# Stage D's casts on ScalarE, one relu and two accumulator sums at other places of their queues

## The chip, the cores and the metric

The kernel runs on one core of one Trainium2 chip. A core has TensorE (PE), VectorE (DVE), ScalarE (ACT), GpSimd (POOL) and SyncE (SP, which here only issues DMAs). Each engine works through its own queue of instructions in order; semaphores make one wait for another. The metric is device time of one execution in microseconds, as the median of several runs.

## The reference

Three layers, one behind the other. Input x is 8 x 3072 x 256 in fp32.

```
X  = rfft(x, axis=1)
Yr = Xr @ w_r - Xi @ w_i + b_r ;  Yi = Xr @ w_i + Xi @ w_r + b_i
Y  = soft threshold of Yr and Yi by 0.01
x  = irfft(Y)                                  # 24576 tokens of 256
x  = (relu(x @ moe_w_in) ** 2) @ moe_w_out     # 256 -> 2048 -> 256, 24576 tokens
logits = x @ phi                               # 32 slots
d  = softmax of logits over the tokens ;  slot_input = d.T @ x
slot_out = per expert (8): relu(slot_input @ w1) @ w2
out = softmax of logits over the slots @ slot_out
```

## The kernel before

The program has three parts: the transform (to about 530 us), the loop over units that holds the two matrix products of the middle layer and the sums over tokens (to about 2065 us), and a short end for the experts and the output. The change touches the loop only.

The 24576 tokens are cut into 32 super-blocks (`sb`) of 768. For each super-block 8 units (`r = n % 8`) are worked through; a unit is 256 of the 2048 hidden channels. A unit multiplies 2 x 2 blocks by seven products, p0 to p6, and each product is three matmuls (128 x 384, line 701), since the numbers are split into a high and a low part: `yh` (the value rounded to fp32r) and `yl` (the rest). The products of one unit are accumulated in two PSUM banks, `psA` and `psX`, with a third, `psZ`, for p4. ScalarE copies `psA` into `psX` (L708 behind p0, L716 behind p5) and `psZ` into SBUF (L722). Of the four results, called parts 0 to 3, parts 1 and 3 are made by VectorE as `psA` or `psX` plus the copy of `psZ` (`add(1)`, `add(3)`, line 735). All are passed through a relu on ScalarE (L739) and squared in place (L743; mostly by GpSimd, part 0 by VectorE). Then TensorE takes them to the logits (`ls`, L754), and VectorE transposes them in pairs into `gt` (`turn(1)` for parts 2 and 3, `turn(0)` for 0 and 1, L747).

The order on all engines is written out by hand in the loop over `n`. In one pass the unit `cur` (n) does p0, p1 and p5, the unit `p1` (n-1) does p4, p6, p2 and p3, and the unit `p2` (n-2) its transpositions and logits. (`p1` and `p2` as objects of the code are units; p1 and p2 as products are methods of the same name.) On TensorE a pass reads p0, p4, p6, p1, p5, p2, p3, logits. p1 needs L708's copy of `psA` into `psX`; p3 writes into `psX` and so needs `add(3)`, which reads it, to be over.

Three things hang in this loop besides:

- Stage D of the next super-block (`stage_d`, the decoding), a generator of which `step(r, k)` takes k pieces at the given r. It does an inverse transform on TensorE (`psY`), copies it to SBUF by ScalarE (four copies, L476; tensors f0 to f3 in the code), and from that makes the seven `yh` and `yl`: seven casts (L480), seven subtractions (L482) and four differences (L464), all on GpSimd.
- The slot run (`into_slots`, L765): at the end of r = 3, TensorE sums the tokens of the super-block before into slots, in four banks (`pz_a`, `pz_x` and two `pz`). The pass r = 4 that follows has another order, and there VectorE adds the banks to `acc` by four `collect` (L770).
- The weights of the slot run: at r = 2 VectorE takes `scores` and `lowest`, ScalarE `exponents` (L821, L822); at r = 3 there is a softmax over the slots (`over_slots`, L778 to L788) with one exponential on ScalarE (L782).

The lines that matter for ScalarE's order at r = 2:

```
step(2, 2)            # the last two copies of stage D
...
p1.p6()
p1.add(3, p1.x)
...
p1.relu(3)
```

Of the kernel before, what the change touches and what calls it, by code (L numbers as in the profile page):

```python
# [103 lines left out]
def fft_moe_kernel(ctx, tc, x, w_r, w_i, b_r, b_i, moe_w_in, moe_w_out, moe2_phi, moe2_w1, moe2_w2,  # L104
                   c_f1, c_bm, c_cm, c_dm, c_st, out):
    nc = tc.nc
# [6 lines left out]
    def f(ap):  # L113
        return ap.bitcast(F32)
# [10 lines left out]
    def drain(it):  # L125
        for _ in it:
            pass
# [312 lines left out]
    def load_z(s):  # L440
        t = zp.tile([128, TB, DM], F32, tag="zt", name=f"zt{s}")
        for g in range(2):
            b, c = divmod(2 * s + g, NC)
            nc.sync.dma_start(t[64 * g:64 * g + N1], zd[b][:, c])
        zt[s] = t

    def stage_d(s, bank, eng):

        yh = yp[s % 2].tile([128, 7, TOK], F32R, tag="yh", name=f"yh{s}")
        yl = yp[s % 2].tile([128, 7, TOK], F32R, tag="yl", name=f"yl{s}")  # L450
        yt[s] = (yh, yl)
        def fill(dh):
            ps = [bank(f"psY{s}_{dh}_{g}")[:, :TOK] for g in range(2)]
            for tt in range(TB):
                for g in range(2):
                    for c in range(2):
                        d = 128 * dh + 64 * c
                        w = slice(64 * g, 64 * g + N1)
                        nc.tensor.matmul(ps[g][64 * c:64 * c + 64, tt::TB], lhsT=zt[s][w, tt, d:d + 64], rhs=dmt[w],  # L459
                                         start=True, stop=True)  # L460
            return ps

        def sub(o, k, m):
            eng.tensor_tensor(out=o, in0=k, in1=m, op=ALU.subtract)  # L464

        if s not in zt:
            load_z(s)
            for _ in range(4):
                yield
        z = zt[s].rearrange("p t d -> p (t d)")  # L470
        f0, f2, f1, f3 = (v[:, o:o + TOK] for v, o in ((wgf, OY), (wgf, OY + TOK), (z, 0), (z, TOK)))
        for dh, ts in enumerate(((f0, f2), (f1, f3))):
            ps = fill(dh)
            yield
            for t, p in zip(ts, ps):
                nc.scalar.copy(t, p)  # L476
                yield
        for j, t, ns in ((0, f0, ((f0, f2, f0),)), (4, f0, ()), (2, f3, ()), (1, f1, ((f2, f3, f2),)),
                         (6, f2, ((f2, f3, f0), (f0, f2, f1))), (5, f2, ()), (3, f0, ())):
            eng.tensor_copy(yh[:, j], t)  # L480
            yield
            eng.tensor_tensor(out=yl[:, j], in0=t, in1=f(yh[:, j]), op=ALU.subtract)  # L482
            yield
            for n in ns:
                sub(*n)
                yield

    XB, XL = 4, NB * NC
    with tc.manual_schedule():
# [155 lines left out]
        def bank(name):  # L645
            return psM.tile([128, 512], F32, tag="g", name=name, bufs=2)

        def bank_a(m, name):
            return psM.tile([128, 512], F32, tag=f"a{m % 2}", name=name)
# [118 lines left out]
        def collect(s, a, p):  # L768

            nc.vector.scalar_tensor_tensor(out=acc[:, :, a], in0=acc[:, :, a], scalar=al[s],  # L770
                                           in1=p.rearrange("p (t n) -> p t n", n=32), op0=ALU.mult, op1=ALU.add)
# [37 lines left out]
        def scores():  # L809
            for h in range(2):  # L810
                w = slice(64 * h, 64 * h + 64)
                nc.vector.tensor_tensor(out=lw[w], in0=lgp[w, HT * h:HT * h + HT], in1=lv[w], op=ALU.add)

        def lowest(s):
            nc.vector.tensor_reduce(out=bx, in_=lw, axis=AX.X, op=ALU.max)
            nc.vector.scalar_tensor_tensor(out=nm[(s + 1) % 3], in0=bx, scalar=-1.0, in1=nm[s % 3], op0=ALU.mult, op1=ALU.min)
# [15 lines left out]
        def turn_rows():  # L832
            nc.vector.transpose(lts, lw)
            return lts.rearrange("p (k n) -> p k n", n=32)
# [52 lines left out]
            nc.tensor.matmul(p, lhsT=ident, rhs=acc.rearrange("p t a n -> p (t a n)")[:, :TOK], start=True, stop=True)  # L887
        units = {}
        NM = NSB * NW
        run = side = None  # L890
        for n in range(NM + 2):
            sb, r = divmod(n, NW)
            s = sb - 1 if sb > 0 and n < NM else None
            cur = units[n] = Unit(n) if n < NM else None
            p1, p2 = units.get(n - 1), units.get(n - 2)

            def step(at, k):

                if side is not None and r == at:
                    for _ in range(k):  # L900
                        next(side, None)

            def route(at):
                return s is not None and r == at

            if run is None:
                if cur:
                    cur.p0()
                step(1, 1)
                if p1:  # L910
                    p1.p4()
                step(1, 1)
                if route(2):
                    scores()
                    lowest(s)
                    exponents(s)
                step(2, 2)
                if p2 and r != 2:
                    p2.turn(1)
                if p1:  # L920
                    p1.p6()
                    p1.add(3, p1.x)
                if route(2):
                    weights(s)
                if p2 and r == 2:
                    p2.turn(1)
                if cur:
                    cur.p1()
                    cur.p5()
                if p2 and r not in (2, 3):  # L930
                    p2.turn(0)
                if p1:
                    p1.p2()
                    p1.add(1, p1.a)
                if p2 and r in (2, 3):
                    p2.turn(0)
                step(1, 1)
                if p1:
                    p1.relu(3)
                    p1.square(3, nc.gpsimd)  # L940
                    p1.p3()
                    p1.square(2, nc.vector if n == NM else nc.gpsimd)
                    p1.relu(1)
                    p1.square(1, nc.vector if n == NM else nc.gpsimd)
                if cur:
                    cur.square(0, nc.vector)
                if route(3):
                    cur.p4()
                    cur.p6()
                    drain(over_slots(turn_rows()))  # L950
                    keep(s, co)
                if p2:
                    p2.logits()
            else:
                sr, ps = run
                run = None
                p2.logits()
                p1.p3()
                p1.square(3, nc.gpsimd)
                p1.square(2, nc.gpsimd)  # L960
                collect(sr, 0, ps[0])
                collect(sr, 1, ps[1])
                cur.p0()
                p1.p2()
                p1.add(1, p1.a)
                collect(sr, 2, ps[2])
                p1.relu(1)
                p1.square(1, nc.gpsimd)
                collect(sr, 3, ps[3])
                cur.p1()  # L970
                cur.p5()
                cur.square(0, nc.gpsimd)
                p2.turn(1)
                p2.turn(0)
            if p1 and p1.s == NSB - 1:
                free_wi(p1.q)
            if n >= NM:
                continue
            if route(1):
                apart()  # L980
            if route(3):
                total(s)
            if r == 0 and sb + 1 < NSB:
                side = stage_d(sb + 1, bank, nc.gpsimd)
                next(side)
            step(2, 3)
            step(3, 10)
            step(4, 1)
            step(5, 2)
            step(6, 3)  # L990
            if r == 5 and sb + 2 < NSB:
                load_z(sb + 2)
            if route(3):
                ps = [bank_a(n + 1, f"pz{s}_a"), bank_x(n + 1, f"pz{s}_x")] + [bank(f"pz{s}_{i}") for i in range(2)]
                into_slots(s, ps)
                cur.add(3, cur.x)
                cur.relu(3)
                run = (s, ps)
            if sb == NSB - 1 and r == 0:
                t = zp.tile([128, TB, DM], F32, tag="zt", name="ez").rearrange("p t d -> p (t d)")  # L1000
                for k in range(2):
                    load_w1(t[:, FE * k:FE * k + FE])
                load_wo()
# [37 lines left out]
        ps = [bank_a(i, f"pz_a{i}") for i in range(2)] + [bank_x(i, f"pz_x{i}") for i in range(2)]  # L1041
# [33 lines left out]
    with ExitStack() as p3, tc.manual_schedule():  # L1075
# [12 lines left out]
        for e in range(e0, NE):  # L1088
            t = wk.tile([128, NX, DM], F32, tag=f"w2{e}", name=f"w2{e}")
# [44 lines left out]
        late = over_slots(lt)  # L1134
# [86 lines left out]
```

## Time and profile before

| | |
|---|---|
| median of 3 runs | 2180.7 us (2176.5, 2181.17, 2180.7) |
| the profiled execution's own time | 2177.24 us |
| its span | 2175.0 us |
| TensorE busy | 2080.6 us (96%) |
| VectorE busy | 1543.0 us (71%) |
| GpSimd busy | 1317.5 us (61%) |
| ScalarE busy | 1277.2 us (59%) |
| mean granted clock of TensorE | 0.977 |

A stretch of the span is best read by the timeline of each engine: start, duration, what ran, and in brackets how long the engine stood idle before it and for whom. The end of a matmul is modelled, so the distance between two starts is the safer number on TensorE. On the other engines instructions overlap a little: the next can start before the duration of the last is over.

### The profile page before, as it was taken

The numbers are of one execution on the slowest core, as the hardware profiler recorded it, in microseconds if no ns is written. First come the engines' busy times: TensorE is split into PE (matmuls) and PEld (weight loads), VectorE is DVE, ScalarE is ACT, GpSimd is POOL, SyncE is SP. The second block draws the span as 40 slices with busy tenths as digits, with TensorE's granted clock in tenths as the row PEclk, the third lists the DMA queues.
The fourth block names the chain that finished last, engine by engine and source line by source line (L and its number), as shares of the span: only waits on it lengthen the run. The fifth ranks groups of instructions, "written<-read, shape, count | busy, mean of one in ns | idle before, by whom it ended". The sixth has DMA issues, their size and how long they took to land.

```text
span 2175.0 us, 55408 instructions
## 1 busy us (share of the span) xinstructions
PE 2080.6 (96%) x22294; PEld 1598.3 (73%) x22294; DVE 1543.0 (71%) x2590; ACT 1277.2 (59%) x2910; POOL 1317.5 (61%) x1583
## 2 busy tenths in 40 slices
PE   8999999998899999999999999999999999999994
PEld 3888888887777777777777777777777777777743
DVE  2677677766577777777777777777777777777743
ACT  2667666754565566566556665655666666556632
POOL 0243344411777777777777777777777777777500
PEclk7999999998999999999999999999999999999995
DMA  8988898863011111111111111111111111111589
GB/s 245 263 242 238 232 231 235 237 152 94 16 36 27 29 36 32 27 27 32 31 29 30 39 27 27 29 34 29 27 41 27 27 27 36 29 27 46 169 302 396
DMA packets 113772, 210.02 MB, mean 97 GB/s; under 512 B 14092, under 2 KB 80908, under 8 KB 107244
## 3 DMA queue, kind: packets, MB, share of 16 engines
q1 hardware_dynamic: 112348, 203.31, 34.6%
q8 instruction: 175, 2.87, 0.6%
q10 hardware_dynamic: 1168, 3.18, 0.4%
q14 instruction: 81, 0.66, 0.1%
HBM read 122.64 MB, written 83.79 MB: 95 GB/s over the span
## 4 chain that ended last, share of the span: by engine, by line
PE 69%; DVE 13%; DMA 5%; ACT 4%; POOL 4%; issue 4%; SPq 1%; DVEq 0%; ACTq 0%; POOLq 0%
PE psX L701 14%; PE psA L701 12%; PE ls L754 7%; DVE gt L747 4%; PE psZ L701 4%; PE pz_a L765 4%; PE psB L247 4%; PE psC L331 4%; PE psY L459 3%; PE pz_x L765 3%; POOL wg L743 3%; PE pz L765 3%; DVE wg L735 3%; PE psA L214 2%; ACT wg L739 2%
## 5 line engine op out<-in xcount | busy, mean ns | idle before, releaser
L743 POOL TENSOR_TENSOR wg<-wg 128x384 f32<-128x384 f32 x797 | 707.3, 910 | 371.3 <-ACT wg L739 368.9
L747 DVE STREAM_TRANSPOSE gt<-wg 128x768 f32<-128x768 f32 x512 | 487.9, 962 | 172.2 <-POOL wg L743 171.9
L739 ACT ACTIVATE wg<-psX 128x384 f32<-128x384 f32 x512 | 251.8, 492 | 269.4 <-PE psX L701 217.6
L701 PE MATMUL psX<-yh,wia 128*128 128x384 f32 x1024 | 364.9, 356 | 39.1 <-DVE wg L735 36.1
L701 PE MATMUL psA<-yh,wia 128*128 128x384 f32 x1024 | 362.2, 359 | 0.0
L739 ACT ACTIVATE wg<-wg 128x384 f32<-128x384 f32 x512 | 267.8, 523 | 139.7 <-DVE wg L735 139.6
L701 PEld LDWEIGHTS psA<-yh,wia 128*128 128x128 f32 x1024 | 192.3, 188 | 103.4 <-DVE wg L735 42.6
L701 PEld LDWEIGHTS psX<-yh,wia 128*128 128x128 f32 x1024 | 192.5, 188 | 95.8 <-DVE wg L735 56.6
L123 POOL TENSOR_TENSOR Sl<-Sf,Sh 128x256 fp32r<-128x256 f32 x96 | 75.4, 786 | 274.2 <-ACT Sh L122 239.8
L754 PE MATMUL ls<-wg 128*32 128x384 f32 x2048 | 219.6, 499 | 0.3 <-DVE wg L743 0.3
L765 PE MATMUL pz_x<-gt,wg 32*32 32x512 f32 x1584 | 209.2, 597 | 0.0
L765 PE MATMUL pz_a<-gt,wg 32*32 32x512 f32 x1584 | 208.9, 596 | 0.0
L765 PE MATMUL pz<-gt,wg 32*32 32x512 f32 x2976 | 203.5, 597 | 0.0
L743 DVE TENSOR_TENSOR wg<-wg 128x384 f32<-128x384 f32 x227 | 195.8, 863 | 7.8 <-ACT wg L739 7.7
L708 ACT COPY psX<-psA 128x384 f32<-128x384 f32 x256 | 119.6, 467 | 120.1 <-PE psA L701 119.7
L701 PE MATMUL psA<-yl,wia 128*128 128x384 f32 x512 | 172.4, 337 | 0.0
L701 PE MATMUL psZ<-yh,wib 128*128 128x384 f32 x512 | 172.1, 336 | 0.0
L701 PE MATMUL psX<-yl,wia 128*128 128x384 f32 x512 | 172.0, 336 | 0.0
L701 PE MATMUL psX<-yh,wib 128*128 128x384 f32 x512 | 171.6, 335 | 0.0
L701 PE MATMUL psA<-yh,wib 128*128 128x384 f32 x512 | 171.5, 335 | 0.0
L735 DVE TENSOR_TENSOR wg<-psX,wg 128x384 f32<-128x384 f32 x256 | 137.1, 536 | 42.5 <-ACT wg L722 32.0
L735 DVE TENSOR_TENSOR wg<-psA,wg 128x384 f32<-128x384 f32 x256 | 136.1, 532 | 41.0 <-PE psA L701 39.0
(211 smaller groups left out, 4807.5 us busy)
## 6 DMA issues: line engine op xcount, KB each, us to landing
bt<-ad SPq DMA_DIRECT2D x96, 256.0 KB
zd<-sc SPq DMA_DIRECT2D x96, 256.0 KB
zt<-zd SPq DMA_DIRECT2D x64, 384.0 KB
xt<-in_x_dram SPq DMA_DIRECT2D x126, 192.0 KB
ad<-sa SPq DMA_DIRECT2D x112, 192.0 KB
out_dram<-ob SPq DMA_DIRECT2D x21, 1024.0 KB
wg<-ed SPq DMA_DIRECT2D x124, 96.0 KB
w<-in_moe_w_dram SPq DMA_DIRECT2D x5, 1024.0 KB
```

Of the source, the lines that this page charges most:

```text
L123: (eng or nc.vector).tensor_tensor(out=lo, in0=v, in1=f(hi), op=ALU.subtract)
L247: nc.tensor.matmul(p[:, dh, :, l], lhsT=t[:, l, 128 * dh:128 * dh + 128], rhs=bm[:, 2 * (u % NU) + l], start=True, stop=True)
L331: nc.tensor.matmul(ps[l][:, v], lhsT=cm[w, (u - 1 + v) % NU, c], rhs=ub[v][w, c], start=c == 0, stop=c == 1)
L459: nc.tensor.matmul(ps[g][64 * c:64 * c + 64, tt::TB], lhsT=zt[s][w, tt, d:d + 64], rhs=dmt[w], start=True, stop=True)
L701: nc.tensor.matmul(p, lhsT=w[:, k, l], rhs=r[:, j], start=start and n == 0, stop=n == 2, skip_group_check=True)
L708: nc.scalar.copy(self.x, self.a)
L735: nc.vector.tensor_tensor(out=self.part(k), in0=p, in1=self.z, op=ALU.add)
L739: nc.scalar.activation(out=t, in_=t if p is None else p, func=AF.Relu)
L743: eng.tensor_tensor(out=t, in0=t, in1=t, op=ALU.mult)
L747: nc.vector.transpose(gt[:, 2 * self.q + a + window(self.s)], self.g[a])
L754: nc.tensor.matmul(lgp[o:o + 32], lhsT=pw[:, 2 * self.q + a], rhs=self.part(k), start=self.first, stop=self.last, skip_group_check=True)
L765: nc.tensor.matmul(ps[a][32 * c:32 * c + 32], lhsT=ee[w, c, k], rhs=gt[w, o:o + NT2, 32 * j:32 * j + 32], start=k == 0, stop=k == NB6 - 1, ...
```

## The change

Four edits, all in stage D and in the loop over units.

1. The seven casts L480 of a super-block's stage D run on ScalarE where stage D ran on GpSimd (31 super-blocks; the first one's stage D runs on VectorE and stays).
2. The last two copies of stage D, which stood early in the pass r = 2, stand at its end, with the first cast behind them (`step(2, 5)`).
3. At r = 2 relu(3) stands right behind the sum add(3).
4. In the pass behind a slot run (r = 4) collect 2 stands ahead of add(1), and collect 3 stands at the end of the pass r = 5.

```diff
--- before.py
+++ after.py
@@ -477,7 +477,7 @@
                 yield
         for j, t, ns in ((0, f0, ((f0, f2, f0),)), (4, f0, ()), (2, f3, ()), (1, f1, ((f2, f3, f2),)),
                          (6, f2, ((f2, f3, f0), (f0, f2, f1))), (5, f2, ()), (3, f0, ())):
-            eng.tensor_copy(yh[:, j], t)
+            (eng.tensor_copy if eng is nc.vector else nc.scalar.copy)(yh[:, j], t)
             yield
             eng.tensor_tensor(out=yl[:, j], in0=t, in1=f(yh[:, j]), op=ALU.subtract)
             yield
@@ -887,7 +887,7 @@
             nc.tensor.matmul(p, lhsT=ident, rhs=acc.rearrange("p t a n -> p (t a n)")[:, :TOK], start=True, stop=True)
         units = {}
         NM = NSB * NW
-        run = side = None
+        run = side = late = None
         for n in range(NM + 2):
             sb, r = divmod(n, NW)
             s = sb - 1 if sb > 0 and n < NM else None
@@ -914,12 +914,13 @@
                     scores()
                     lowest(s)
                     exponents(s)
-                step(2, 2)
                 if p2 and r != 2:
                     p2.turn(1)
                 if p1:
                     p1.p6()
                     p1.add(3, p1.x)
+                if p1 and r == 2:
+                    p1.relu(3)
                 if route(2):
                     weights(s)
                 if p2 and r == 2:
@@ -936,7 +937,8 @@
                     p2.turn(0)
                 step(1, 1)
                 if p1:
-                    p1.relu(3)
+                    if r != 2:
+                        p1.relu(3)
                     p1.square(3, nc.gpsimd)
                     p1.p3()
                     p1.square(2, nc.vector if n == NM else nc.gpsimd)
@@ -952,7 +954,7 @@
                 if p2:
                     p2.logits()
             else:
-                sr, ps = run
+                sr, ps = late = run
                 run = None
                 p2.logits()
                 p1.p3()
@@ -962,11 +964,10 @@
                 collect(sr, 1, ps[1])
                 cur.p0()
                 p1.p2()
+                collect(sr, 2, ps[2])
                 p1.add(1, p1.a)
-                collect(sr, 2, ps[2])
                 p1.relu(1)
                 p1.square(1, nc.gpsimd)
-                collect(sr, 3, ps[3])
                 cur.p1()
                 cur.p5()
                 cur.square(0, nc.gpsimd)
@@ -983,7 +984,9 @@
             if r == 0 and sb + 1 < NSB:
                 side = stage_d(sb + 1, bank, nc.gpsimd)
                 next(side)
-            step(2, 3)
+            if late and r == 5:
+                collect(late[0], 3, late[1][3])
+            step(2, 5)
             step(3, 10)
             step(4, 1)
             step(5, 2)
```

VectorE from the slot run of super-block 1 on, the passes r = 4 and r = 5, as a piece of the difference. L770 is a collect (`pz_a`, `pz_x`, `pz_0`, `pz_1` are its banks 0 to 3), L735 with `psA` is add(1), with `psX` add(3), L747 a transposition, L743 the square of part 0; the number behind `psA_` or `psX_` is the group of channels of the unit:

```order
 L770 SCALAR_TENSOR_TENSOR acc<-acc,al_7570,pz_x 128x16x32
+L770 SCALAR_TENSOR_TENSOR acc<-acc,al_7570,pz_0_7693 128x16x32
 L735 TENSOR_TENSOR wg<-psA_1_7618,wg 128x384
-L770 SCALAR_TENSOR_TENSOR acc<-acc,al_7570,pz_0_7693 128x16x32
+L747 STREAM_TRANSPOSE gt<-wg 128x768 x3
+L735 TENSOR_TENSOR wg<-psX_2_7806,wg 128x384
+L747 STREAM_TRANSPOSE gt<-wg 128x768
+L735 TENSOR_TENSOR wg<-psA_2_7805,wg 128x384
+L743 TENSOR_TENSOR wg<-wg 128x384
 L770 SCALAR_TENSOR_TENSOR acc<-acc,al_7570,pz_1_7694 128x16x32
-L747 STREAM_TRANSPOSE gt<-wg 128x768 x3
```

Collect 2 (`pz_0`) moved up by one instruction, ahead of add(1), and collect 3 (`pz_1`) down by seven, behind the square of r = 5; transpositions and add(3) stand two instructions closer to add(1).

ScalarE in the pass r = 2 of super-block 1, from the second exponential to the copy L708 of r = 3. L476 are the two copies of stage D, L739 from `wg` to `wg` is a relu of part 3 or 1, L739 from `psX` of part 0 or 2. Before:

```order
L822 ACTIVATE al_7570<-nm_74,nm_75 128x1
L476 COPY zt_7304<-psY_1_0_7505 128x384
L476 COPY zt_7304<-psY_1_1_7506 128x384
L739 ACTIVATE wg<-psX_0_7556 128x384
L716 COPY psX_0_7556<-psA_0_7555 128x384
L739 ACTIVATE wg<-wg 128x384
L739 ACTIVATE wg<-psX_7_7475 128x384
L739 ACTIVATE wg<-wg 128x384
L708 COPY psX_1_7619<-psA_1_7618 128x384
```

and of the kernel changed:

```order
L822 ACTIVATE al_7570<-nm_74,nm_75 128x1
L739 ACTIVATE wg<-wg 128x384
L739 ACTIVATE wg<-psX_0_7556 128x384
L716 COPY psX_0_7556<-psA_0_7555 128x384
L739 ACTIVATE wg<-psX_7_7475 128x384
L739 ACTIVATE wg<-wg 128x384
L476 COPY zt_7304<-psY_1_0_7505 128x384
L476 COPY zt_7304<-psY_1_1_7506 128x384
L480 CAST yh_7438<-wg 128x384
L708 COPY psX_1_7619<-psA_1_7618 128x384
```

Relu(3) moved up by four, to the place behind the exponential; the two copies moved down behind the other relus, and the cast stands between them and L708.

ScalarE at the end of r = 3, beside the slot run, as a piece of the difference (L722 copies `psZ`, L782 is the softmax's exponential, L480 are the casts, L739 from `wg` the relu(3) of r = 3, L739 from `psX` its relu(2)):

```order
 L722 COPY wg<-psZ_1_7657 128x384
 L782 ACTIVATE wg<-wg 128x192
+L480 CAST yh_7438<-wg 128x384
+L480 CAST yh_7438<-zt_7304 128x384 x2
+L480 CAST yh_7438<-wg 128x384
 L739 ACTIVATE wg<-wg 128x384
 L739 ACTIVATE wg<-psX_1_7619 128x384
```

Four casts came in between the exponential and relu(3).

## Rows read from the trace of the kernel before

**Rows 1.** Waits of TensorE, whole span: total us, times, longest us.

```profile
PE psX L701 <- DVE wg L735: 36.1, 63, 6.0
```

**Rows 2.** Timeline of TensorE, one period: start us, us, engine line op [idle before].

```profile
888.34 0.44 PE L701 MATMUL psX<-yh,wia 128*128 128x384 f32 x1
...
889.85 0.34 PE L701 MATMUL psA<-yh,wia 128*128 128x384 f32 x1
890.62 0.44 PE L701 MATMUL psX<-yh,wia 128*128 128x384 f32 x1 [0.44 <-DVE wg L735]
...
906.48 0.34 PE L701 MATMUL psA<-yh,wia 128*128 128x384 f32 x1
907.32 0.44 PE L701 MATMUL psX<-yh,wia 128*128 128x384 f32 x1 [0.51 <-DVE wg L735]
907.60 0.34 PE L701 MATMUL psX<-yl,wia 128*128 128x384 f32 x1
```

**Rows 3.** Timeline of VectorE, the same period.

```profile
884.31 0.56 DVE L735 TENSOR_TENSOR wg<-psX,wg 128x384 f32<-128x384 f32 x1
...
887.38 1.05 DVE L743 TENSOR_TENSOR wg<-wg 128x384 f32<-128x384 f32 x1
889.15 0.98 DVE L747 STREAM_TRANSPOSE gt<-wg 128x768 f32<-128x768 f32 x1 [0.72 <-POOL wg L743]
890.05 0.52 DVE L735 TENSOR_TENSOR wg<-psX,wg 128x384 f32<-128x384 f32 x1
...
902.35 0.56 DVE L735 TENSOR_TENSOR wg<-psA,wg 128x384 f32<-128x384 f32 x1 [1.19 <-PE psA L701]
902.82 1.40 DVE L770 SCALAR_TENSOR_TENSOR acc<-acc,al,pz 128x512 f32<-128x512 f32 x2
904.14 2.69 DVE L747 STREAM_TRANSPOSE gt<-wg 128x768 f32<-128x768 f32 x3
906.75 0.52 DVE L735 TENSOR_TENSOR wg<-psX,wg 128x384 f32<-128x384 f32 x1
...
912.73 0.55 DVE L743 TENSOR_TENSOR wg<-wg 128x384 f32<-128x384 f32 x1
```

**Rows 4.** Timeline of ScalarE, the same period.

```profile
884.95 0.83 ACT L476 COPY zt<-psY 128x384 f32<-128x384 f32 x2
...
886.59 0.53 ACT L739 ACTIVATE wg<-wg 128x384 f32<-128x384 f32 x1
...
887.82 0.47 ACT L708 COPY psX<-psA 128x384 f32<-128x384 f32 x1
...
894.68 0.36 ACT L782 ACTIVATE wg<-wg 128x192 f32<-128x192 f32 x1 [1.89 <-DVE wg L780]
...
901.36 0.49 ACT L739 ACTIVATE wg<-psX 128x384 f32<-128x384 f32 x1 [2.74 <-PE psX L701]
```

**Rows 5.** Timeline of GpSimd, the same period.

```profile
887.19 2.71 POOL L743 TENSOR_TENSOR wg<-wg 128x384 f32<-128x384 f32 x3 [3.64 <-ACT wg L739]
...
895.28 0.50 POOL L480 CAST yh<-wg 128x384 fp32r<-128x384 f32 x1
895.86 1.01 POOL L482 TENSOR_TENSOR yl<-wg,yh 128x384 fp32r<-128x384 f32 x1
...
900.02 1.00 POOL L464 TENSOR_TENSOR wg<-zt,wg 128x384 f32<-128x384 f32 x1
...
903.74 3.18 POOL L743 TENSOR_TENSOR wg<-wg 128x384 f32<-128x384 f32 x4
```

**Rows 6.** Groups of ScalarE, by form: xcount | busy us, mean ns | idle before.

```profile
L708 ACT COPY psX<-psA 128x384 f32<-128x384 f32 x256 | 119.6, 467 | 120.1 <-PE psA L701 119.7
...
L122 ACT CAST wib<-s 128x384 fp32r<-128x384 f32 x8 | 4.2, 524 | 0.0
```

**Rows 7.** Chain in order of time, last super-block, r = 3: start us, us, what.

```profile
2033.28 1.04 PE psA L701 x6
2034.32 0.57 PE psX L701 x3
```

## The prediction

> **What bounds the kernel now.** I read the waits of TensorE first. One kind stands out: the product into `psX` waits for the sum of line 735 on VectorE, 63 times, 36.1 us in all, the longest 6.0 us [rows 1]. The longest one is in the first super-block; the other 62, 30.1 us, are two for each of the 31 super-blocks with a slot run. The loop is otherwise an almost gapless stream of matmuls, so what can be won is in these two places, plus the long stall.
>
> Then TensorE in order of time through one period, from 888 to 908 us [rows 2]. Free-running matmuls of three follow each other at 0.173 us (six take 1.04 us in [rows 7]). Place A is r = 5, the unit after the slot run: the last matmul of p2 starts at 906.48, the first of p3 at 907.32 instead of 906.66, and the second comes 0.28 behind it instead of 0.18. So A costs 0.66 + 0.10 = 0.76 us. Place B is r = 3: 889.85 to 890.62 is 0.77 where 0.18 would do, and with the slow second matmul (by the shape of A) B costs 0.59 + 0.10 = 0.69 us.
>
> Next, who is late. At A it is VectorE alone [rows 3]: sum add(1) at 902.35, the collects 2 and 3 from 902.82 to 904.14, three transpositions from 904.14 in a row, then add(3) at 906.75, and p3 starts when that ends. At B add(3) comes at 890.05, behind a transposition that could only start at 889.15 because GpSimd's squares started late, at 887.19 [rows 3, 5]. They waited for relu(3), which ScalarE began at 886.59, behind the two copies of stage D that began at 884.95 [rows 4]. The last super-block has no stage D, and there p3 (psX, 0.57 us for three) follows p2 with almost no gap [rows 7]. That is the cross-check for B: take the copies from in front of the relu and B's wait goes.
>
> **The change part by part.** *Collects (place A).* Collect 2 moves ahead of add(1). VectorE idles there for 1.19 us until p2 is done [rows 3], and a collect is 0.70 us (1.40 for two), so it costs nothing; without that idle time it would cost its 0.70. Collect 3 goes behind the square of r = 5. The 1.32 us between 902.82 and 904.14 so leaves the chain: transpositions from 902.82, add(3) at 905.43 instead of 906.75, ended near 906.0. TensorE is ready for p3 at 906.66. What is late next is TensorE itself, with 0.66 us to spare, and A is gone. Collect 3 brings back 0.70 of the 1.32 us in r = 5, so VectorE reaches r = 6 no later than now. The PSUM bank that it holds longer is wanted next by stage D at the next r = 0. Term 1: 31 x 0.76 = **23.6 us**.
>
> *Relu(3) and the two copies (place B).* Relu(3) takes the place of the copies, near 885.0; its sum (884.31, 0.56 us) has just ended [rows 3, 4]. GpSimd's first square then starts 1.6 us earlier, near 885.6. The second needs relu(2), which stands three instructions behind relu(3) in the new queue; the four instructions from 884.95 to 886.59 and the three from 886.59 to 887.82 both go at 0.41 us each, so it starts near 886.3 and ends at 886.8, and the second square ends near 887.7. The transposition is then free to go as soon as VectorE is through with the square at 887.38 (1.05 us), at 888.4 instead of 889.15; add(3) follows 0.9 later at 889.3 and ends near 889.85.
>
> *The first cast.* The same two copies, and behind them the first of the casts, now stand just ahead of the copy L708 of r = 3. ScalarE has no idle time from 884.95 to that copy at 887.82, so the copy comes later by one cast. No row has this cast on ScalarE; the nearest is L122 of the same shape, 0.52 us long [rows 6], and neighbours follow at 0.41. I take 0.43, with 0.3 and 0.6 as ends. The copy ends at 887.82 + 0.47 = 888.29 now and p1 of r = 3 starts at 888.34: p1 has no slack, and goes to 888.77. From there p2 and p3 run freely: p3 at 890.03 + 0.43 = 890.46 instead of 890.62, and no slow restart. So B gives back 0.16 + 0.10 = 0.26 us of its 0.69, and the wait of p3 on VectorE turns into a shorter one of p1 on ScalarE. Term 2, for the 30 super-blocks with both stage D and a slot run: 30 x 0.26 = **7.8 us** (bounds: 30 x 0.69 = 20.7 if the cast finds room, -9 if p1 is late by 1.0).
>
> The rows show VectorE's square at 887.38 taking 1.05 us beside GpSimd's squares, and 0.55 at 912.73 where it starts first [rows 3, 5]. The Trainium skill (SBUF — State Buffer, section Who interferes with whom) says that a VectorE instruction with two SBUF inputs and a GpSimd instruction that reads SBUF exclude each other, and the later one is blocked until the first ends. The trace agrees in the longer duration. By that rule GpSimd's third square, now moved up beside it, could hold VectorE's once more; this case is rival 1.
>
> *The four casts of r = 3.* They lie behind the exponential of the softmax, which starts at 894.68 [rows 4]; with p2 of r = 3 some 0.4 us later, and add(1) behind it, I put it at 894.9. First cast 895.25 to 895.75, and GpSimd's subtraction near 895.8, now 895.86. After that GpSimd no longer does the casts: three subtractions and the difference for the last cast at 1.0 us each end at 899.8 instead of 901.0 [rows 5]. The last cast waits for that on ScalarE, and relu(3) and relu(2) of r = 3 and the copy L708 of r = 4 are queued behind it: 899.85, relu(3) 900.3, free at 900.7. Relu(2) now starts at 901.36, in the new time 901.1. 0.4 us are left; cost nothing. GpSimd's four squares, now from 903.74, start over 1 us earlier, so they don't hold the transpositions of term 1.
>
> *The casts at r = 5 and 6.* Each comes just ahead of a copy L708, before which ScalarE idles 0.47 us on average (120.1 us for 256) [rows 6]. 0.43 fits. The cover is thin, and 0.1 us too much, twice in 30 super-blocks, would cost 6 us.
>
> *First super-block.* No slot run gives ScalarE a gap there. GpSimd's queue holds up p3 by 6.0 us today [rows 1]. Five casts of 0.5 to 0.6 us (895.28 to 895.86 is one) leave it, at most 2.9 us, but ScalarE now waits for GpSimd with the copy for p1 queued behind, so most of the stall only moves to p1. I take 1 us of gain, between -2 and +3.
>
> Sum: 23.6 + 7.8 + 1 = 32.4 us. The profiled execution took 2177.2 us, so 2144.8. The median of the runs is 2180.7 with the lowest at 2176.5, so a median may lie up to 4 us above such a sum.
>
> **The rivals.** *1. The ScalarE queue eats term 2.* The cast costs 0.6 or more, relu(3) starts later than 885.0, the square at 887.38 is held for another 0.85 us as the rule above has it (add(3) would end near 890.7, 0.25 after TensorE asks), or the thin cover at r = 5 and 6 is missed. Then only term 1 stays: 2153, down to a loss of 9 us with 2162. For it: ScalarE has no idle time at B. Against it: the durations on both sides are steady.
>
> *2. Room found.* Where the copy L708 is not delayed, B goes wholly: 2177.2 - 23.6 - 20.7 - 1 = 2132. Against it: no idle time before 887.82.
>
> *3. The wait only changes its name.* At A the third transposition needs two squares of GpSimd. They start at 903.74 today; if the subtractions, which now wait for ScalarE's casts, put them back to 904.2, add(3) is as late as today, term 1 is nothing, and at 904.5 p3 is 0.26 us later than today, which takes what B gives: 2177. Against it: GpSimd gets rid of four casts before that point.
>
> *4. Slower.* ScalarE stands still in r = 3 for the last cast. It decides at the start of that cast: 900.25 is the latest without harm, and each us behind it is a us of TensorE in each of 30 super-blocks, since p1 of r = 4 waits for the copy behind it. If three subtractions with their casts keep the pace of today's pairs (4.74 us from 895.28 to 900.02) because the two engines hand over one by one, the difference starts at 900.5, ends at 901.5, and the cast is 1.3 us too late: 30 x 1.3 = 39 us, 2184. Against it: three of the casts are queued in a row and need not wait for a subtraction.
>
> **How the numbers follow.** The forecast (2140 to 2150) 0.60; rival 1 (2153 to 2162) 0.17; rival 2 (2132) 0.08; rival 3 (2177) 0.09; rival 4 (2184) 0.06. Faster by over 0.2% (4.4 us, about what a measurement of this kernel can tell from no change) is the first three, 0.85; within it rival 3, 0.09; slower rival 4, 0.06. The range goes from 2133 to 2163: forecast, rival 1 and a part of rival 2.
>
> **What would show it.** In the waits of TensorE the 62 waits for VectorE's sum should fall to next to none, and about 30 short ones of `psX` for ScalarE's copy L708 (0.4 to 0.5 us, at r = 3) come up. The period should fall by some 1.0 us. On VectorE add(3) of r = 5 comes near 1.3 us sooner after add(1) than now. On ScalarE the last of the casts in r = 3 starts before relu(2) is wanted. The forecast is wrong if A keeps a gap (the third transposition waits for GpSimd), or if p1 of r = 4 waits longer for L708 than now. The loop's count of matmuls and its clock should not change.

## The result and the profile after

| | before | changed |
|---|---|---|
| median of four runs | 2180.5 us | 2148.4 us |
| runs | 2176.5 to 2181.2 | 2144.3 to 2152.5 |
| span of the profiled execution | 2175.0 us | 2145.0 us |
| GpSimd busy | 1317.5 us | 1208.9 us |
| ScalarE busy | 1277.2 us | 1359.4 us |

The ratio is 0.9856, with a 95% interval of 0.9834 to 0.9879. The forecast was 2145.

The waits of TensorE in the changed kernel (total us, times, longest), to be held against [rows 1]:

```profile
PE psX L701 <- ACT psX L708: 13.0, 32, 4.9
...
PE psX L701 <- DVE wg L735: 1.0, 1, 1.0
```

The 63 waits for VectorE's sum are down to one, in the end of the loop, where it also stood before. In their place stand 32 for ScalarE's copy L708: one of 4.9 us in the first super-block, one of 0.6 us at the loop's start, which is not new, and 30 of 0.24 to 0.37 us at r = 3, one in each super-block with both stage D and a slot run.

TensorE through a period of the changed kernel, places B and A, and the same matmul one period on, against [rows 2]:

```profile
883.48 0.34 PE L701 MATMUL psX<-yh,wib 128*128 128x384 f32 x1
884.06 0.44 PE L701 MATMUL psX<-yh,wia 128*128 128x384 f32 x1 [0.24 <-ACT psX L708]
...
885.58 0.34 PE L701 MATMUL psA<-yh,wia 128*128 128x384 f32 x1
885.75 0.34 PE L701 MATMUL psX<-yh,wia 128*128 128x384 f32 x1
...
901.49 0.34 PE L701 MATMUL psA<-yh,wia 128*128 128x384 f32 x1
901.66 0.33 PE L701 MATMUL psX<-yh,wia 128*128 128x384 f32 x1
...
930.76 0.45 PE L701 MATMUL psX<-yh,wia 128*128 128x384 f32 x1 [0.24 <-ACT psX L708]
```

p3 follows p2 without a gap at both places (885.58 to 885.75, 901.49 to 901.66). What is left is p1 at r = 3: 883.48 to 884.06 is 0.58 where 0.18 would do, so it costs 0.40 us, though the wait listed is 0.24. The period is 930.76 - 884.06 = 46.70 us. In the kernel before the same two rows of p3 at r = 3 stand at 890.62 and, a period on, at 938.39:

```profile
938.39 0.44 PE L701 MATMUL psX<-yh,wia 128*128 128x384 f32 x1 [0.46 <-DVE wg L735]
```

That is 47.77, so a period is 1.07 us shorter; the prediction had some 1.0.

VectorE in the timeline of the changed kernel, for [rows 3]:

```profile
882.70 0.68 DVE L743 TENSOR_TENSOR wg<-wg 128x384 f32<-128x384 f32 x1
883.30 0.96 DVE L747 STREAM_TRANSPOSE gt<-wg 128x768 f32<-128x768 f32 x1
...
897.36 0.56 DVE L735 TENSOR_TENSOR wg<-psA,wg 128x384 f32<-128x384 f32 x1 [0.53 <-PE psA L701]
897.83 2.69 DVE L747 STREAM_TRANSPOSE gt<-wg 128x768 f32<-128x768 f32 x3
900.44 0.52 DVE L735 TENSOR_TENSOR wg<-psX,wg 128x384 f32<-128x384 f32 x1
```

add(3) at r = 5 now starts 3.08 us behind add(1) (900.44 - 897.36), before 4.40 (906.75 - 902.35): 1.32 less, as worked out, and TensorE is the late one there. At B the transposition at 883.30 follows the square at once.

GpSimd in the same timeline, its four squares ahead of the transpositions of A, for [rows 5]:

```profile
897.14 3.19 POOL L743 TENSOR_TENSOR wg<-wg 128x384 f32<-128x384 f32 x4
```

They now start 0.22 us ahead of add(1) (897.36), before 1.39 behind it (903.74 to 902.35 in [rows 5] and [rows 3]): 1.61 us earlier, so no transposition at A waits for them.

ScalarE in the same timeline, for [rows 4]:

```profile
880.27 0.51 ACT L739 ACTIVATE wg<-wg 128x384 f32<-128x384 f32 x1
...
883.08 0.55 ACT L480 CAST yh<-wg 128x384 fp32r<-128x384 f32 x1
883.50 0.51 ACT L708 COPY psX<-psA 128x384 f32<-128x384 f32 x1
...
894.49 0.51 ACT L480 CAST yh<-wg 128x384 fp32r<-128x384 f32 x1 [3.30 <-POOL wg L464]
...
896.31 0.49 ACT L739 ACTIVATE wg<-psX 128x384 f32<-128x384 f32 x1 [0.89 <-PE psX L701]
```

Relu(3) stands where the copies stood. The cast begins at 883.08 and the copy behind it at 883.50: it costs the queue 0.42 us, though it is 0.55 long. The last cast of r = 3 waits 3.30 us for GpSimd, and relu(2) comes to its turn 0.89 us before it is wanted, so rival 4 did not come about. The casts at r = 5 and 6 found room too: ScalarE still idles 0.27 and 0.21 us before the copies L708 behind them (903.95 and 908.61).

### The profile page after: what moved, and what is told of

It is laid out like the page before. It is cut to its first block, busy times and chain, and to the rows that moved or that the text cites. A ratio compares the mean times of both kernels' runs of the same rounds, so it can differ in the third digit from the quotient of the medians.

```text
span 2145.0 us, 55341 instructions
## 1 busy us (share of the span) xinstructions
PE 2066.0 (96%) x22294; PEld 1602.4 (75%) x22294; DVE 1540.8 (72%) x2590; ACT 1359.4 (63%) x3127; POOL 1208.9 (56%) x1366
## 4 chain that ended last, share of the span: by engine, by line
PE 77%; ACT 9%; DVE 6%; DMA 4%; issue 2%; POOL 1%; SPq 1%; ACTq 0%; DVEq 0%; POOLq 0%
PE psX L701 16%; PE psA L701 15%; PE ls L754 6%; PE psZ L701 5%; PE psB L247 4%; ACT wg L739 4%; PE psC L331 4%; PE pz_a L765 4%; PE psY L459 3%; PE pz L765 3%; PE pz_x L765 3%; DVE acc L770 3%; PE psA L214 2%; PE psL L117 2%; PE psL L118 2%
## 5 line engine op out<-in xcount | busy, mean ns | idle before, releaser
L743 POOL TENSOR_TENSOR wg<-wg 128x384 f32<-128x384 f32 x797 | 703.8, 907 | 407.6 <-ACT wg L739 407.5
L747 DVE STREAM_TRANSPOSE gt<-wg 128x768 f32<-128x768 f32 x512 | 487.2, 961 | 124.9 <-POOL wg L743 124.6
L701 PE MATMUL psX<-yh,wia 128*128 128x384 f32 x1024 | 358.1, 350 | 16.2 <-ACT psX L708 13.0
L739 ACT ACTIVATE wg<-psX 128x384 f32<-128x384 f32 x512 | 251.3, 491 | 186.3 <-PE psX L701 166.3
L739 ACT ACTIVATE wg<-wg 128x384 f32<-128x384 f32 x512 | 267.1, 522 | 23.3 <-DVE wg L735 23.2
L743 DVE TENSOR_TENSOR wg<-wg 128x384 f32<-128x384 f32 x227 | 207.4, 914 | 7.2 <-ACT wg L739 7.0
L482 POOL TENSOR_TENSOR yl<-wg,yh 128x384 fp32r<-128x384 f32 x155 | 157.0, 1013 | 56.9 <-ACT yh L480 56.9
L708 ACT COPY psX<-psA 128x384 f32<-128x384 f32 x256 | 120.3, 470 | 99.1 <-PE psA L701 96.7
L735 DVE TENSOR_TENSOR wg<-psX,wg 128x384 f32<-128x384 f32 x256 | 137.4, 537 | 52.4 <-ACT wg L722 42.7
L735 DVE TENSOR_TENSOR wg<-psA,wg 128x384 f32<-128x384 f32 x256 | 136.5, 533 | 49.7 <-PE psA L701 49.0
```

Source lines behind the costliest of these rows:

```text
L701: nc.tensor.matmul(p, lhsT=w[:, k, l], rhs=r[:, j], start=start and n == 0, stop=n == 2, skip_group_check=True)
L708: nc.scalar.copy(self.x, self.a)
L735: nc.vector.tensor_tensor(out=self.part(k), in0=p, in1=self.z, op=ALU.add)
L739: nc.scalar.activation(out=t, in_=t if p is None else p, func=AF.Relu)
L743: eng.tensor_tensor(out=t, in0=t, in1=t, op=ALU.mult)
L747: nc.vector.transpose(gt[:, 2 * self.q + a + window(self.s)], self.g[a])
```

## The experiments

Each is compared with runs of the kernel before on the same chip, whose medians were 2179.6, 2178.6 and 2180.1 us in the three sets. Where medians of different sets are held against each other, the period of the loop stands beside them: the time from the logits of one r = 3 to those of the next, as the median over 29 super-blocks of the trace. It is 47.77 us before and 46.71 us in the changed kernel.

**The collects alone.** Onto the kernel before:

```diff
-                p1.add(1, p1.a)
                 collect(sr, 2, ps[2])
+                p1.add(1, p1.a)
                 p1.relu(1)
                 p1.square(1, nc.gpsimd)
-                collect(sr, 3, ps[3])
...
+            if late and r == 5:
+                collect(late[0], 3, late[1][3])
```

> The kernel before with one part of the change alone: collect 2 ahead of add(1), collect 3 at the end of r = 5. Casts, copies and relu stay where they were. Theory 1 (place A is VectorE's queue alone): A goes wholly, 31 x 0.76 = 23.6 us, 2157. Theory 2 (behind VectorE's queue stands GpSimd's): in this kernel the four squares of GpSimd still start at 903.74 on the clock of before, two of them take 1.6 us, so the third transposition starts at 905.35 instead of 904.6, add(3) ends near 906.8 and p3 still waits 0.15 + 0.10 us; 31 x 0.5 = 15.8 us, 2165. B stays as it was in both, 0.44 us of wait in each super-block.

Measured: 2166.35 us, ratio 0.9943 (0.9926 to 0.9959), a gain of 13.2 us. Place A in its timeline, first GpSimd:

```profile
666.31 3.18 POOL L743 TENSOR_TENSOR wg<-wg 128x384 f32<-128x384 f32 x4
```

VectorE:

```profile
667.96 0.98 DVE L747 STREAM_TRANSPOSE gt<-wg 128x768 f32<-128x768 f32 x1 [0.72 <-POOL wg L743]
668.86 0.52 DVE L735 TENSOR_TENSOR wg<-psX,wg 128x384 f32<-128x384 f32 x1
```

And TensorE:

```profile
669.06 0.34 PE L701 MATMUL psA<-yh,wia 128*128 128x384 f32 x1
669.43 0.45 PE L701 MATMUL psX<-yh,wia 128*128 128x384 f32 x1
669.72 0.34 PE L701 MATMUL psX<-yl,wia 128*128 128x384 f32 x1
```

Theory 2 holds. The collects are out of the chain, but the third transposition waits 0.72 us for the squares that GpSimd starts at 666.31. p3 comes 0.37 behind p2's last matmul instead of 0.18, and its second matmul 0.29 later: 0.30 us of A's 0.76 stay. So VectorE is not alone at A: GpSimd's squares stand 0.72 us behind its queue, and term 1 needs GpSimd to be early as well.

**All but the collects.** The changed kernel with the lines above put back.

> The changed kernel with the two collects back at their old places. Theory 1 (the parts add): A stays with its wait of 0.5 us for VectorE's sum, B turns into the short wait of p1 for L708; only term 2 is left, 30 x 0.26 = 8 us, plus about 1.6 of the first super-block: 2171. Rival (the casts' move off GpSimd is what shortens A): A's wait for VectorE's sum falls too, and the time comes near the 2148 of the changed kernel.

Measured: 2169.31 us, 0.9955 (0.994 to 0.9969), a gain of 10.3 us. Its waits of TensorE:

```profile
PE psX L701 <- DVE wg L735: 16.7, 32, 1.0
PE psX L701 <- ACT psX L708: 12.9, 32, 4.9
```

A is back with its wait of 0.5 us in each super-block, and B is the short wait for L708. From here to the changed kernel the collects bring 20.9 us (2169.3 - 2148.4; the period falls from 47.46 to 46.71, 0.75), against 13.2 when made alone (47.77 to 47.32, 0.45).

**All seven casts back on GpSimd**, and **only the first of them**:

```diff
-            (eng.tensor_copy if eng is nc.vector else nc.scalar.copy)(yh[:, j], t)
+            eng.tensor_copy(yh[:, j], t)
```

```diff
-            (eng.tensor_copy if eng is nc.vector else nc.scalar.copy)(yh[:, j], t)
+            (eng.tensor_copy if eng is nc.vector or j == 0 else nc.scalar.copy)(yh[:, j], t)
```

> The changed kernel with all seven casts back on GpSimd; the order of everything else is that of the changed kernel. Theory 1 (the first cast on ScalarE costs p1 of r = 3 its 0.4 us and the rest of the casts earn nothing): the wait of p1 for L708 goes, GpSimd's squares of r = 3 start near 902.4 on the clock of before since relu(3) of r = 2 is early, A stays gone, the period falls by another 0.4 us: 2148 - 13 = 2135. Rival (the casts have to leave GpSimd for A to go): the third transposition waits for GpSimd's squares, p3 at r = 5 waits 0.2 us or more for VectorE's sum in each super-block, and the time is 2140 to 2155.

> The changed kernel with only the first of the seven casts (the one between the two copies and L708 of r = 3) back on GpSimd; the other six stay on ScalarE. Theory 1: p1's wait of 0.24 us by the profile (0.4 us between starts) for L708 goes in 30 super-blocks, 30 x 0.43 = 13 us, 2135, and nothing else moves. Rival (another thing holds r = 3 there, GpSimd's later subtraction or the copies themselves): a wait of p1 or p3 stays at r = 3 and the time is within 5 us of 2148.

Measured: 2135.20 us (0.9799, 0.9783 to 0.9814) with all seven on GpSimd, 2134.68 us (0.98, 0.9773 to 0.9827) with the first alone. Both beat the changed kernel by 13 to 14 us. The waits of TensorE, first with all seven on GpSimd:

```profile
PE psX L701 <- DVE wg L735: 6.9, 2, 6.0
...
PE psX L701 <- ACT psX L708: 0.6, 1, 0.6
```

and with only the first:

```profile
PE psX L701 <- ACT psX L708: 6.0, 2, 5.4
...
PE psX L701 <- DVE wg L735: 1.0, 1, 1.0
```

In both the short waits at r = 3 are gone, and nothing has come for them in these passes; the period is 46.29 us in both, 0.42 shorter. Only the stall in the first super-block is longer than the changed kernel's 4.9 us. So the first cast on ScalarE costs 13 us, and the other six there bring nothing that can be measured once relu and copies stand where the change has put them. What is left at A with all seven on GpSimd is one wait of 0.17 us on VectorE, which does not reach TensorE:

```profile
760.39 0.98 DVE L747 STREAM_TRANSPOSE gt<-wg 128x768 f32<-128x768 f32 x1 [0.17 <-POOL wg L743]
```

**Which of relu and copies it is.** The changed kernel with relu(3) back behind L716:

```diff
-                if p1 and r == 2:
-                    p1.relu(3)
...
-                    if r != 2:
-                        p1.relu(3)
+                    p1.relu(3)
```

> The changed kernel with relu(3) of r = 2 back behind the copy L716 (the two stage D copies and the first cast stay at the end of r = 2). Theory 1 (moving the copies away is enough, the relu's own move adds nothing): relu(3) starts 0.9 us later than in the changed kernel, GpSimd's second square still ends before VectorE is through with its square of part 0, no wait of p3 for VectorE's sum comes back, 2148 +- 4. Rival (the relu's place is what removes B): p3 of r = 3 waits again for VectorE's sum, by the profile 0.2 to 0.45 us in each of 30 super-blocks, 2155 to 2165.

with the copies back:

```diff
+                step(2, 2)
                 if p2 and r != 2:
...
-            step(2, 5)
+            step(2, 3)
```

> The changed kernel with the two stage D copies back at their old place at r = 2, ahead of relu(3), which keeps its new place ahead of relu(0); the first cast stays alone ahead of L708. Theory 1 (relu(3) 0.7 us later does no harm, and L708 stays late by the cast as ScalarE has the same work in front of it): 2148 +- 4, with the same wait of p1 for L708. Rival (the copies in front of relu(3) are the whole of B): p3 of r = 3 waits again for VectorE's sum, 2155 to 2165.

and with both:

> The changed kernel with both the two stage D copies and relu(3) of r = 2 back at their old places; casts on ScalarE and collects as changed. Since either of the two moves alone gave the full 2148, Theory 1 says that one of them is needed, and without both GpSimd's first square is late again, p3 of r = 3 waits for VectorE's sum as in the kernel before while p1 also waits for L708: of the 0.69 us of B nothing comes back, 2148 + 8 = 2156. Rival (neither is needed; only GpSimd without its first cast counts): 2148.

Measured: 2147.67 us (0.9857, 0.9842 to 0.9871) with the relu back, 2147.90 us (0.9861, 0.9845 to 0.9878) with the copies back, 2155.40 us (0.9882, 0.9864 to 0.9899) with both. Either move alone is enough, and without both 7 us are lost (0.32 us of each period, 47.03 against 46.71). With both back, GpSimd's squares start late, and p3 of r = 3 comes 0.37 behind p2 and its second matmul 0.29 later:

```profile
746.69 0.34 PE L701 MATMUL psA<-yh,wia 128*128 128x384 f32 x1
747.06 0.44 PE L701 MATMUL psX<-yh,wia 128*128 128x384 f32 x1
747.35 0.34 PE L701 MATMUL psX<-yl,wia 128*128 128x384 f32 x1
```

At A, however, nothing is left in this kernel. GpSimd's four squares start 0.08 us behind add(1) (758.80), with the collects alone 1.38 behind it (664.93 to 666.31), and p3 follows p2 without a gap. First GpSimd, then TensorE:

```profile
758.88 3.18 POOL L743 TENSOR_TENSOR wg<-wg 128x384 f32<-128x384 f32 x4
```

```profile
762.93 0.33 PE L701 MATMUL psA<-yh,wia 128*128 128x384 f32 x1
763.11 0.33 PE L701 MATMUL psX<-yh,wia 128*128 128x384 f32 x1
```

This kernel differs from the one with the collects alone only in the seven casts. So without the moves of copies and relu the casts on ScalarE are worth 11 us (2166.4 to 2155.4; the period falls from 47.32 to 47.03, by the 0.30 us that was left of A). With those moves made, GpSimd is early enough at A already, 0.83 us behind add(1) with all casts on it, and the casts add nothing there.

**Copies and relu alone.** The kernel before with these two moves and nothing else (`step(2, 5)` at the end, casts on GpSimd, collects as before).

> The kernel before with the copies and relu(3) at their new places and nothing else: casts on GpSimd, collects at their old places. Theory 1 (B is the ScalarE order alone, and A is untouched): B's 0.69 us goes in 30 super-blocks, 21 us, A keeps its wait of 0.5 us for VectorE's sum: 2179 - 21 = 2158. With the 13.4 us that the collects alone gave it does not reach the 2135 of both together, since GpSimd's squares also come earlier: the difference of some 10 us is what the two give each other. Rival (GpSimd's casts hold B too): a wait at r = 3 stays, 2165 or more.

Measured: 2159.09 us, 0.9903 (0.9882 to 0.9924), a gain of 21.0 us: 0.70 us in each of 30 super-blocks, the 0.69 by which B was sized. With 13.2 from the collects alone this makes 34, and both together (all casts on GpSimd) gain 44.4. The 10 us between are what each does for the other: the moves bring GpSimd's squares forward at A too, and close the 0.30 us that the collects alone leave there (31 x 0.30 = 9).

**Two more subtractions ahead of the last cast of r = 3**, for rival 4 of the prediction:

```diff
+            for _ in range(2 if j == 1 and s > 1 else 0):
+                eng.tensor_tensor(out=yl[:, 3], in0=t, in1=f(yh[:, j]), op=ALU.subtract)
```

> The changed kernel with two subtractions more on GpSimd (128 x 384, 1.0 us each, into a tile that is overwritten later) ahead of the difference for which the last cast of r = 3 waits, in the 30 super-blocks with a slot run. Theory 1 (rival 4 of the prediction is a real mechanism with a threshold): ScalarE stood idle for 0.89 us between relu(3) and relu(2) of r = 3, so 2.0 us more on GpSimd make p1 of r = 4 wait 1.1 us longer for L708: 30 x 1.1 = 33 us, 2181. Theory 2 (GpSimd's time beside the slot run is free, its lateness only counts at the transposition of r = 5): p1 keeps its place, p3 of r = 5 waits about 0.5 us for VectorE's sum, 2148 + 15 = 2163 or less.

Measured: 2172.65 us, 0.9972 (0.9962 to 0.9983), 24.3 us more than the changed kernel. ScalarE at r = 4 (the lines of the code stand two lower):

```profile
709.38 0.51 ACT L480 CAST yh<-wg 128x384 fp32r<-128x384 f32 x1 [5.36 <-POOL wg L464]
...
710.60 0.48 ACT L710 COPY psX<-psA 128x384 f32<-128x384 f32 x1
```

and TensorE:

```profile
709.82 0.34 PE L703 MATMUL psA<-yh,wia 128*128 128x384 f32 x1
711.13 0.45 PE L703 MATMUL psX<-yh,wia 128*128 128x384 f32 x1 [0.98 <-ACT psX L710]
```

Theory 1: the copy is late, and p1 comes 1.31 us behind the last matmul ahead of it, in the changed kernel 0.41 (896.98 to 897.39). 0.90 of the 2.08 us came through, so 1.2 were slack, not the 0.9 that I had read from ScalarE's idle time alone: relu(2) and the copy behind it also close up (0.37 apart here, 0.57 there). 30 x 0.90 = 27 us; the median shows 24.3. The mechanism of the rival is real; in the changed kernel the cast was in time.

**Spreading stage D in the first super-block**, with the first cast on GpSimd:

```diff
-            step(3, 10)
-            step(4, 1)
-            step(5, 2)
-            step(6, 3)
+            for at, k in ((3, 4), (4, 3), (5, 3), (6, 3), (7, 2)) if sb == 0 else ((3, 10), (4, 1), (5, 2), (6, 3)):
+                step(at, k)
```

> The kernel with the first cast on GpSimd, and besides the pieces of stage D in the first super-block spread out, 4, 3, 3, 3 and 2 at r = 3 to 7 instead of 10, 1, 2 and 3 at r = 3 to 6, since there is no slot run beside which to do them. Theory 1 (the first super-block's stall is the pile of ten pieces in GpSimd's and ScalarE's queues): the stall of 4.9 us and the slow matmuls behind it, some 1.7 us, go for the most part, 5 to 6 us less than with the first cast on GpSimd alone: 2129. Rival (GpSimd is short of time there however the pieces lie): stalls of 1 to 2 us in several units instead, no gain.

Measured: 2127.52 us, 0.9769 (0.9754 to 0.9784). The stall in the first super-block is gone (waits of TensorE, whole span):

```profile
PE psX L701 <- DVE wg L735: 1.0, 1, 1.0
...
PE psX L701 <- ACT psX L708: 0.6, 1, 0.6
```

That is 7.2 us below the kernel with the first cast moved back, which was measured in another set. The stall is 5.4 of them; the rest is of the size that the slow matmuls behind the stall had cost (0.32 us apart instead of 0.17), but no run shows that part by itself. This kernel is faster than the kernel before and the changed one.

**p0 ahead of p3 behind the slot run**, on top of that:

```diff
                 p2.logits()
-                p1.p3()
-                p1.square(3, nc.gpsimd)
-                p1.square(2, nc.gpsimd)
                 collect(sr, 0, ps[0])
                 collect(sr, 1, ps[1])
                 cur.p0()
+                p1.p3()
+                p1.square(3, nc.gpsimd)
+                p1.square(2, nc.gpsimd)
                 p1.p2()
```

> The fastest kernel so far (first cast on GpSimd, pieces spread in the first super-block) with p0 of r = 4 and its copy L708 ahead of p3 and relu(2) of r = 3 in the pass behind the slot run. Theory: the 0.41 us between the starts of the last matmul of p2 and the first of p1 there is L708, that begins only when p0 is through; with p0 three matmuls earlier the copy is over when p1 is due, 31 x 0.25 = 8 us less, 2120. Rival: p0 now waits for collect 0, which frees its bank, and collect 1, 0.1 to 0.5 us, and nothing is won: 2125 to 2130.

Measured: 2127.96 us, 0.9755 (0.9735 to 0.9775): no change against the kernel that it was built on. TensorE from the logits of r = 3 to those of r = 4, in this kernel's timeline:

```profile
746.94 0.85 PE L754 MATMUL ls<-wg 128*32 128x384 f32 x8
747.80 0.44 PE L701 MATMUL psA<-yh,wia 128*128 128x384 f32 x1
...
749.30 0.33 PE L701 MATMUL psA<-yh,wia 128*128 128x384 f32 x1
749.47 0.33 PE L701 MATMUL psX<-yh,wia 128*128 128x384 f32 x1
...
751.38 0.34 PE L701 MATMUL psZ<-yh,wib 128*128 128x384 f32 x1
751.71 0.44 PE L701 MATMUL psX<-yh,wib 128*128 128x384 f32 x1
...
754.55 0.85 PE L754 MATMUL ls<-wg 128*32 128x384 f32 x8
```

and the copy for which p6 waits, from ScalarE:

```profile
751.20 0.46 ACT L716 COPY psX<-psA 128x384 f32<-128x384 f32 x1
```

The gap at p1 is gone: it starts 0.17 behind p2. Another has come behind three more products (p5, p0 and p4), where p6 waits for the copy L716, which ends at 751.66, and starts 0.33 behind p4 with a slow second matmul. From logits to logits it is 754.55 - 746.94 = 7.61 us. In the kernel that this one was built on the same two rows start at 745.04 and 752.65, 7.61 as well: one gap for another. p0 hardly waited for its bank, since it starts at 747.80, when the logits end (746.94 + 0.85).

## Why the prediction was right

The sum had three terms. *Term 1* was 0.76 us for each slot run; from the kernel without the collects to the changed one the period falls by 0.75, and the medians give 20.9 us, 0.67 for each of 31. The step that carried more than it seemed to is the sentence that GpSimd's squares start over 1 us earlier. That A is VectorE's alone was not so: at GpSimd's old start, with the collects moved alone, the gain is 13.2 us, and what stays is a wait by the mechanism of rival 3. The step held, with 1.61 us in the changed kernel, and for the reason given: the casts alone bring 1.30 of it (from 1.38 to 0.08 us behind add(1)), and the moves of copies and relu alone, which the prediction did not name for A, would have been enough as well.

*Term 2* was 0.26 us for 30 super-blocks, the difference between a wait that goes (0.69) and one that comes (0.43). The wait that comes measures 0.40 in the trace of the changed kernel and 13.7 us, 0.46 each, when the first cast is taken off ScalarE again (2148.4 - 2134.7; 0.42 by the period). The wait that goes measures 0.70 each (copies and relu alone). The net is as forecast (0.31 by the period of the kernel without the collects), and so is the wait of p1 named for it, except that the profile lists it with 0.24 us and not with 0.4 to 0.5: the listed wait is shorter than the delay between starts.

*Term 3*, the first super-block, was 1 us. There the stall moved from p3 to p1, as said, and fell from 6.0 to 4.9 us by the profile [rows 1].

One reading was off: of the 62 waits that the prediction gives two each to 31 super-blocks, 31 are at A, 30 at B, and one of 1.0 us is at the end of the loop, where it stays. The sum does not change by it, since term 2 counts 30 super-blocks.

The span fell by 30.0 us and not by more since the changed kernel's profiled execution came later into the loop: the 60 matmuls of the first `psY` in the loop start at 539.13 before and at 542.38 after, 3.25 us later, in a part of the program that the change does not touch. From there to the end of the span the changed kernel is 33 us shorter, against 32.4 in the sum. Runs of one kernel differ by as much as 8 us, and this head is one place that varies: in the profiles of all these kernels, whose head is the same, those matmuls start between 538.7 and 543.9.

Two smaller steps were off without moving the sum. The slack ahead of relu(2) at r = 3 was taken as 0.4 us and is 0.89, as a step of VectorE's softmax took 0.36 us instead of 0.97 (below). And the hint that VectorE's square at B could be held longer by GpSimd came out the other way: 0.68 us at 882.70 instead of 1.05.

## What to carry to other kernels

Where an engine waits for a chain over two others, write down for each place the time at which it would be ready itself; a move is worth the distance to the next one late, not the wait that it removes, and two moves can need each other (13 and 21 us alone, 44 together). Work that is moved into an engine's idle time counts where it stands in that engine's queue: of seven casts the one just ahead of a copy that TensorE waits for cost 13 us of what the rest of the change had gained. The other six cost nothing and brought nothing, but only because another part of the change did the same work; without that part the casts were worth 11 us. So after a change of several parts, undo each part alone, and undo together those that can stand in for each other; here the kernel without its named main part is the better one.

## What the runs showed of the hardware

Two operations of VectorE with both inputs in SBUF became shorter, since they met GpSimd's squares at another moment. The first is the subtraction of the softmax (L780): 0.97 us before, beside squares of GpSimd, and 0.36 in the changed kernel, where it starts as GpSimd's squares end and GpSimd then waits for ScalarE's cast. GpSimd's row and VectorE's, before and then after:

```profile
892.50 2.83 POOL L743 TENSOR_TENSOR wg<-wg 128x384 f32<-128x384 f32 x3
893.67 0.97 DVE L780 TENSOR_TENSOR wg<-wg 128x192 f32<-128x192 f32 x1
```

```profile
886.47 2.71 POOL L743 TENSOR_TENSOR wg<-wg 128x384 f32<-128x384 f32 x3 [0.34 <-ACT wg L739]
889.20 0.36 DVE L780 TENSOR_TENSOR wg<-wg 128x192 f32<-128x192 f32 x1
```

The other is the square of r = 2, 1.05 to 0.68 us. Here GpSimd squares beside it in both kernels. Before, VectorE's square starts 0.19 us behind the first of GpSimd's (887.19 to 887.38); in the changed kernel 0.57 us behind one (882.13 to 882.70), so that less of GpSimd's is still to come:

```profile
882.13 1.93 POOL L743 TENSOR_TENSOR wg<-wg 128x384 f32<-128x384 f32 x2 [0.45 <-ACT wg L739]
```

With the copies at their old place no instruction of GpSimd is at work when the square starts (883.02 in that kernel), and it takes 0.52.

The Trainium skill (SBUF — State Buffer, section Who interferes with whom) says that a VectorE instruction with two SBUF inputs contends with a GpSimd instruction that reads SBUF, and that the port pair which the two share is an exclusive lock. These durations agree. It is the moment that counts here and not the engine that casts: with only relu(3) back at its old place, and all seven casts on ScalarE, the subtraction again meets GpSimd's squares (from 885.45 on, 2.81 us) and takes

```profile
887.49 0.98 DVE L780 TENSOR_TENSOR wg<-wg 128x192 f32<-128x192 f32 x1
```

That kernel is as fast as the changed one (2147.67 us), so no wait of TensorE hung on these 0.6 us.
